# Transposing the ds tiles of an attention backward loop by three DMAs a block instead of two

## The chip, the cores and the metric

One core of a Trainium2 chip. The metric is the device time of one execution in microseconds (us). The engines: TensorE (PE in the profile, PEld its weight loads), VectorE (DVE), ScalarE (ACT), GpSimd (POOL), SyncE (SP). SyncE computes nothing here; it issues nearly all DMAs, one after the other, in program order.

## The reference, cut to what matters

A parallel block, attention plus a gated feed-forward, run forward and then differentiated:

```python
def _fwd_reference(A_x, ...):
    xn = _layernorm(A_x)
    return A_x + attention(xn, A_wqkv, A_wo) + swiglu(xn, B_w_gate, B_w_up, B_w_down)
# S = 2048 tokens, D = 448, H = 16 heads of 28, F = 1792
# result: the output, and the gradients of x and of five weights
```

The attention backward needs, for each head and each pair of a query tile and a key chunk, `ds` (the gradient of the scores) twice: as it is, for dk, and transposed, for dq.

## The kernel before: the parts concerned

The backward loop runs 512 steps. A step is one query tile of 128 rows against a key chunk of 512 columns for two heads; four steps (qi = 0 to 3) are a block. `row` makes the score and dP matmuls. `ew` makes exp on ScalarE and `ds` on VectorE, into buffers that hold two tiles each:

```python
def dst_dma(b, ds, qi):
    if qi == 2:
        SP.dma_start_transpose(out=dsT[b][:, 2]..., in_=ds[:, 0]...)        # one tile, L826
        return
    dsT[b] = bk.tile([P, 4, 2, 4, P], BF16, name="dsT", bufs=3)
    SP.dma_start_transpose(out=dsT[b][:, 0:2]..., in_=ds[:]...)             # two tiles, L830

def ew(k):
    ...                                                                     # exp
    if qi % 2 == 0:
        dss[k - 1] = dss[k] = kq.tile([P, 2, 2, 512], BF16, name="ds_sb", bufs=5)
    ds = dss[k - 1]
    for j in range(2):
        DVE.tensor_tensor(out=ds[:, qi % 2, j], in0=dps..., in1=est..., op=ALU.mult)   # L845
    if qi == 1 or qi == 2 and b < NB // 4 - 1:
        dst_dma(b, ds, qi)
```

Tile 3 of a block is transposed on TensorE instead (`tr_unit`, L900). `dq_unit(b)` uses all four transposed tiles ten steps after tile 2 was written. With five buffers, a ds buffer is written again when the fifth newer pair of tiles comes, and that write must wait until the DMA has read the old tiles.

The same SyncE queue carries the loop's other traffic: prefetch loads "dripped" in at some 100 KB a step (L767) and stores of results (L800).

```python
def drop():                       # once a step
    ...
    while slow and credit > 0:
        _, _, o, i = slow.pop(0)
        SP.dma_start(out=o, in_=i)
        credit -= size(o)
```

One ds tile is 128 x 1024 bf16, 256 KB; a typical load piece is 256 KB too.

The softmax here doesn't subtract the row's maximum and nothing guards it: scores larger than these inputs give would overflow.

## Time and profile before

| | before |
|---|---|
| median of 3 runs | 1472.74 us (1466.82 to 1473.25) |
| PE, ACT, DVE busy | 91%, 86%, 79% of the span |
| backward loop, block 0 to 126 | 789.8 us, 6.27 us a block |
| two-tile issue / one-tile issue on SyncE, median | 3.04 / 1.25 us |

A "block" is timed in the trace from the end of one block's fourth ds multiply (of eight, two a tile; the fourth completes tile 1) to the next block's. An issue's duration is how long SyncE is held by it, not how long the data move: in the queue kernel of experiment 1 the two-tile issue at 29.03 us held SyncE for 1.84 us, and its last packet started 3.76 us after it. The lines themselves are in the prediction below.

### The profile page before, as it was taken

The numbers are of one execution on the slowest core, as the hardware profiler recorded it, in microseconds if no ns is written. First come the engines' busy times: TensorE is split into PE (matmuls) and PEld (weight loads), VectorE is DVE, ScalarE is ACT, GpSimd is POOL, SyncE is SP. The second block draws the span as 40 slices with busy tenths as digits, with TensorE's granted clock in tenths as the row PEclk, the third lists the DMA queues.
The fourth block names the chain that finished last, engine by engine and source line by source line (L and its number), as shares of the span: only waits on it lengthen the run. The fifth ranks groups of instructions, "written<-read, shape, count | busy, mean of one in ns | idle before, by whom it ended". The sixth has DMA issues, their size and how long they took to land. (4 is left out here: it accounts for less than half of the span.)

```text
span 1468.9 us, 34341 instructions
## 1 busy us (share of the span) xinstructions
PE 1338.7 (91%) x12647; PEld 544.8 (37%) x12708; DVE 1153.9 (79%) x1997; ACT 1262.4 (86%) x2193; POOL 361.8 (25%) x486
## 2 busy tenths in 40 slices
PE   5889999989999999888899989999999999999996
PEld 2333333333333333333333433433343444344343
DVE  6667756656667767497888878888889999899988
ACT  5789988988989998687888879899989999888974
POOL 6464514553344444010001101101001011010005
PEclk9999999999999999998999999999999999999998
DMA  5797957696778685699999999999999999999961
GB/s 151 147 210 179 223 118 179 165 197 155 167 160 190 145 184 125 206 198 199 214 204 196 214 204 189 210 203 216 212 195 194 206 217 217 199 194 206 193 140 59
DMA packets 697664, 271.14 MB, mean 185 GB/s; under 512 B 616128, under 2 KB 672152, under 8 KB 697496
## 3 DMA queue, kind: packets, MB, share of 16 engines
q1 hardware_dynamic: 692520, 262.82, 86.7%
q0 software_dynamic: 3568, 5.83, 1.8%
q8 instruction: 100, 1.64, 0.5%
q14 instruction: 68, 0.56, 0.1%
q10 hardware_dynamic: 1408, 0.30, 0.1%
HBM read 65.04 MB, written 59.90 MB: 85 GB/s over the span
## 5 line engine op out<-in xcount | busy, mean ns | idle before, releaser
L845 DVE TENSOR_TENSOR ds_sb<-db,e_sb 128x512 bf16<-128x512 f32 x1024 | 648.4, 685 | 68.6 <-PE db L818 22.6
L837 ACT ACTIVATE e_sb<-sb 128x512 bf16<-128x512 f32 x1024 | 554.1, 609 | 60.3 <-PE db L818 43.8
L611 ACT ACTIVATE eT<-s_w 128x1024 bf16<-128x1024 f32 x256 | 263.7, 1030 | 48.6 <-PE s_ps L608 45.8
L613 ACT ACTIVATE eT<-s_ps 128x512 bf16<-128x512 f32 x512 | 280.2, 611 | 0.0
L818 PE MATMUL db<-kd,qd 32*128 32x512 bf16 x1024 | 239.9, 385 | 19.5 <-DVE ds_sb L845 18.7
L810 PE MATMUL sb<-kd,qd 32*128 32x512 bf16 x1024 | 210.9, 389 | 7.5 <-DMA qd<-QD_d 3.7
L964 POOL TENSOR_TENSOR dq_acc<-dq_acc,dq_st 128x256 f32<-128x256 f32 x64 | 46.4, 724 | 588.6 <-ACT dq_st L962 588.6
L905 ACT COPY dsT<-db 128x1024 bf16<-128x1024 bf16 x128 | 130.0, 1016 | 37.1 <-PE db L900 36.5
L922 PE MATMUL acc<-ds_sb,qd 128*32 128x512 bf16 x1024 | 161.4, 392 | 0.0
L918 PE MATMUL acc<-e_sb,qd 128*32 128x512 bf16 x1024 | 159.4, 392 | 1.3 <-DVE dw_o L527 1.3
L379 POOL TENSOR_TENSOR nn<-nn,ag 128x512 f32<-128x512 f32 x56 | 71.2, 1272 | 253.9 <-DVE ag L377 245.4
L608 PE MATMUL s_ps<-QQ,KK 32*128 32x512 bf16 x512 | 125.5, 385 | 3.9
L1132 PE MATMUL genb<-wguT,dau_c 128*128 128x448 bf16 x448 | 117.5, 355 | 6.3 <-ACT dq_st L962 3.8
L608 PE MATMUL s_w<-QQ,KK 32*128 32x512 bf16 x512 | 100.3, 387 | 13.2 <-ACT eT L611 10.2
L810 PEld LDWEIGHTS <-qd 32*128 32x128 bf16 x1024 | 48.3, 91 | 152.6 <-issue 140.6
L420 PE MATMUL gen<-xn_t,f_sp 128*128 128x448 bf16 x416 | 91.8, 354 | 2.6 <-DVE nn L394 1.7
L949 PE MATMUL genb<-dsT,kd 128*32 128x256 bf16 x2048 | 80.9, 279 | 3.5 <-DVE y L1084 1.8
L420 PEld LDWEIGHTS <-f_sp 128*128 128x128 bf16 x640 | 55.7, 98 | 76.4 <-issue 31.7
L900 PE MATMUL db<-ident_bf,ds_sb 128*128 128x128 bf16 x1032 | 82.1, 225 | 0.9 <-DVE ds_sb L845 0.9
L900 PEld LDWEIGHTS <-ds_sb 128*128 128x128 bf16 x1032 | 70.6, 101 | 28.6 <-issue 10.3
L450 PE MATMUL gen<-eT,VS 128*32 128x512 bf16 x1024 | 68.0, 382 | 6.0 <-DVE nn L394 3.8
L380 POOL TENSOR_TENSOR nn<-nn,tt 128x512 f32<-128x512 f32 x56 | 72.0, 1286 | 4.4
(163 smaller groups left out, 1872.0 us busy)
## 6 DMA issues: line engine op xcount, KB each, us to landing
F_d<-hda SPq DMA_DIRECT2D x56, 384.0 KB
dau_c<-F_d SPq DMA_DIRECT2D x56, 256.0 KB
h_c<-F_d SPq DMA_DIRECT2D x24, 256.0 KB
qd<-QD_d SPq DMA_DIRECT2D x24, 256.0 KB
dc<-dqkvT_d SPq DMA_DIRECT2D x12, 384.0 KB
dsT<-ds_sb SPq DMA_TRANSPOSE x255
wT_d<-wT_f SPq DMA_DIRECT2D x14, 256.0 KB
KD_d<-qk_sp SPq DMA_DIRECT2D x7, 512.0 KB
```

The source lines that it names most:

```text
L420: PE.matmul(ps[:, :D], lhsT=fsp[fc][:, t // 4, w, t % 4, :], rhs=rhs[:, t, :], start=(t == 0), stop=(t == NT - 1))
L608: PE.matmul(sp4[hh], lhsT=KK[g][r:r + HP, kt * P:(kt + 1) * P], rhs=QQ[g][r:r + HP, qsl], start=True, stop=True, tile_position=(r, 0))
L611: ACTE.activation(out=e2[0][:], in_=wide[:], func=ACT.Exp, scale=SCALE)
L613: ACTE.activation(out=e2[1][:, j], in_=sp4[2 + j], func=ACT.Exp, scale=SCALE)
L810: PE.matmul(s_ps[:], lhsT=qside[g, qc][r:r + HP, 0, qi * P:(qi + 1) * P], rhs=kside[g, kc][r:r + HP, 0, :], start=True, stop=True, tile_po ...
L818: PE.matmul(d_ps[:], lhsT=qside[g, qc][r:r + HP, 1, qi * P:(qi + 1) * P], rhs=kside[g, kc][r:r + HP, 1, :], start=True, stop=True, tile_po ...
L837: ACTE.activation(out=est[k][:, j], in_=sps.pop((k, j))[:], func=ACT.Exp, scale=SCALE)
L845: DVE.tensor_tensor(out=ds[:, qi % 2, j], in0=dps.pop((k - 1, j))[:], in1=est[k - 1][:, j], op=ALU.mult)
L900: PE.transpose(ps[:, c, :], ds[:, qi % 2, c // 4, (c % 4) * P:(c % 4 + 1) * P], ident_bf[:])
L905: ACTE.copy(out=o, in_=ps[:])
L918: PE.matmul(a[r:r + HP, :], lhsT=sp4[:, 1, r:r + HP], rhs=e[:, j, :], start=first, stop=last, tile_position=(0, r), skip_group_check=True)
L922: PE.matmul(a[r:r + HP, :], lhsT=sp4[:, 0, r:r + HP], rhs=ds[:, qi % 2, j, :], start=first, stop=last, tile_position=(0, r), skip_group_ch ...
```

## The change

Its intent: each of the three tiles goes out as soon as it is written, so its transpose starts earlier and its buffer is free earlier. It costs one more DMA a block. The bytes, the matmuls and the transposes on TensorE stay the same.

```diff
     def dst_dma(b, ds, qi):
-        if qi == 2:
-            SP.dma_start_transpose(out=dsT[b][:, 2]..., in_=ds[:, 0]...)
-            return
-        dsT[b] = bk.tile([P, 4, 2, 4, P], BF16, name="dsT", bufs=3)
-        SP.dma_start_transpose(out=dsT[b][:, 0:2]..., in_=ds[:]...)
+        if qi == 0:
+            dsT[b] = bk.tile([P, 4, 2, 4, P], BF16, name="dsT", bufs=3)
+        SP.dma_start_transpose(out=dsT[b][:, qi]..., in_=ds[:, qi % 2]...)
 ...
-            if qi == 1 or qi == 2 and b < NB // 4 - 1:
+            if qi < 2 or qi == 2 and b < NB // 4 - 1:
```

More of the change, by code (lines that the diff above doesn't have):

```diff
@@ L824, in dst_dma @@
     def dst_dma(b, ds, qi):
-        if qi == 2:
-            SP.dma_start_transpose(out=dsT[b][:, 2].rearrange("p j kt s -> p (j kt) s"),
-                                   in_=ds[:, 0].rearrange("p j k -> p (j k)"))
-            return
-        dsT[b] = bk.tile([P, 4, 2, 4, P], BF16, name="dsT", bufs=3)
-        SP.dma_start_transpose(out=dsT[b][:, 0:2].rearrange("p q j kt s -> p (q j kt) s"),
-                               in_=ds[:].rearrange("p q j k -> p (q j k)"))
+        if qi == 0:
+            dsT[b] = bk.tile([P, 4, 2, 4, P], BF16, name="dsT", bufs=3)
+        SP.dma_start_transpose(out=dsT[b][:, qi].rearrange("p j kt s -> p (j kt) s"),
+                               in_=ds[:, qi % 2].rearrange("p j k -> p (j k)"))
     def ew(k):
```

## The prediction

> **What bounds the kernel now.** I read four views in this order: the page's slices, the waits of VectorE, windows around the longest of those waits, and the timeline of SyncE's DMA issues.
>
> The change touches only the backward attention loop, which runs from about 620 to 1430 us: 128 blocks of four query tiles, some 6.27 us a block ((1414.0 - 624.2) us between the same multiply of block 0 and block 126, over 126). The slices say that TensorE, ScalarE and the DMA engines are all nearly full there.
>
> ```profile
> PE   5889999989999999888899989999999999999996
> DVE  6667756656667767497888878888889999899988
> ACT  5789988988989998687888879899989999888974
> PEclk9999999999999999998999999999999999999998
> DMA  5797957696778685699999999999999999999961
> ```
>
> A tuned loop like this is not set by one engine. What the change can win is what TensorE loses to DMA, so I ask who waits for the transposes. Of VectorE's waits from 620 to 1430 us (total us, times, longest us):
>
> ```profile
> DVE ds_sb L845 <- PE db L818: 22.6, 57, 1.7
> DVE ds_sb L845 <- DMA dsT<-ds_sb: 15.9, 11, 2.5
> ```
>
> The second line is the one: the multiply that writes a ds tile stood still 11 times because the transposing DMA had not yet read what lay in that buffer before. The longest eight of these waits lie at 668, 680, 690, 711, 768, 854, 888 and 1262 us: mostly the first third of the loop. The worst one, first TensorE's timeline, then windows around it (busy us of each engine, granted clock, DMA share, GB/s):
>
> ```profile
> 665.51 0.39 PE L818 MATMUL db<-kd,qd 32*128 32x512 bf16 x1
> 668.56 0.58 PE L818 MATMUL db<-kd,qd 32*128 32x512 bf16 x1 [2.66 <-DVE ds_sb L845]
> ```
>
> ```profile
> 640.00:667.00 27.00, 24.52 (x295) 11.50 (x292) 22.96 (x38) 25.37 (x49) 0.72 (x1) 1.00 0.99 201
> 667.00:674.00 7.00, 5.40 (x46) 2.02 (x46) 3.87 (x7) 3.31 (x6) 0.23 (x1) 0.52 0.91 185
> 674.00:740.00 66.00, 58.41 (x623) 23.52 (x623) 54.49 (x89) 54.24 (x100) 7.01 (x10) 0.95 1.06 206
> ```
>
> VectorE's wait becomes 2.66 us of TensorE idle, and then the granted clock falls from 1.00 to 0.52 for 7 us. Windows over 711 to 715, 769 to 773, 854 to 858 and 1264 to 1268 us each show 0.57, right behind the waits at 711, 768, 854 and 1262. So a wait for a transpose is paid about twice.
>
> Why are the transposes late? SyncE issues them; L830 is two tiles in one DMA, L826 one tile:
>
> ```profile
> 652.81 0.57 SPq L767 DMA_DIRECT2D wd_sb<-in_B_w_down_dram  x1
> 653.43 0.48 SPq L767 DMA_DIRECT2D h_c<-F_d  x1
> 654.01 3.21 SPq L830 DMA_TRANSPOSE dsT<-ds_sb  x1
> 657.27 1.43 SPq L800 DMA_DIRECT2D out_dram<-dqT  x2
> 658.80 2.03 SPq L826 DMA_TRANSPOSE dsT<-ds_sb  x1
> 660.92 0.52 SPq L800 DMA_DIRECT2D dqkvT_d<-dkv  x1
> 661.50 0.97 SPq L767 DMA_DIRECT2D h_c<-F_d  x2
> 662.57 3.27 SPq L830 DMA_TRANSPOSE dsT<-ds_sb  x1
> ```
>
> There is no hole between these lines: SyncE's queue is full. The two tiles that go out at 662.57 us were ready at 653.85 us (end of block 5's fourth multiply), so the queue is 8.7 us behind its data. Followed in the timeline from block to block, this lag grows from 2.6 us (block 0) to 13.0 us (block 7), is cut by VectorE's waits, stands at 5 to 11 us up to 880 us, rises again near 1060 and 1255 us, and is 0.03 us from 1350 us on. The rows of the two lines give min/median/max in ns:
>
> ```profile
> L830 SPq DMA_TRANSPOSE dsT<-ds_sb x128: 1746/3044/4773, 626.8 to 1419.8; - x128
> L826 SPq DMA_TRANSPOSE dsT<-ds_sb x127: 1232/1252/2486, 629.8 to 1415.9; - x127
> ```
>
> One tile costs 1.25 us nearly always; two together cost not 2.5 but 3.04.
>
> **What the Trainium skill says.** "Perfetto Trace Analysis", section "DMA Instruction — HWDGE (DVE, Sync)": the profiled window runs from satisfied semaphores to a free sequencer, so it is descriptor generation, not data movement, and the DMA engines start before it is over when more descriptors are made than the buffer holds. That fits: two tiles alone in a quiet queue take 1.75 us, behind copies in flight up to 4.77 us, as if the issue must wait until part of itself has drained, while one tile fits. The same page, "What 'DMA-bound' means": a sequencer track that is solid DMA slices is a bound of its own. The trace agrees from 640 to 720 us: issues fill 96% of SyncE's time. The same page, "DMA Optimizations", has it both ways: batch small transfers, yet splitting may let some start sooner if the DMA engines are generally idle. They are not idle here (slices of 9), which is the case against the change. "TensorE: Matmul & The Clock Gate", "What's actually happening": an idle window of about 3.4 us halves the clock. The trace agrees on the halving, though 2.66 us of idle was enough.
>
> **The change part by part.**
> 1. Removed: per block one two-tile issue. Added: two one-tile issues. The same bytes in the same 256-byte packets move. At the medians: 2 x 1.25 - 3.04 = -0.54 us of SyncE time a block. Per block from 640 to 720 us: before, 3.26 (mean of L830 there) + 1.34 (mean of L826) + 3.1 copies x 0.56 + 5 gaps of 0.05 = 6.6 us, against some 5.87 us that blocks 1 to 7 took before the waits began; so the lag must grow 0.7 us a block. After: 3 x 1.30 (mean of one-tile issues, my choice between 1.25 and 1.34) + 1.74 + 0.30 = 5.9 us: even with the block. From 720 to 900 us the same sum gives 3.12 + 1.48 + 1.45 + 0.25 = 6.3 before and about 5.7 after. The lag stops growing and mostly vanishes.
> 2. Moved: the first tile's transpose is asked for one step (about 1.4 us) earlier, and the second no longer ends with its partner. By the code, the buffer that held tiles 0 and 1 is written again nine steps later (about 13.2 us). Minus 3.3 us of issue and an assumed 2.2 us until landed, a lag of 7.7 us is tolerated now; with 1.25 us of issue, 9.8 us.
> 3. Added: the dsT tile is taken one step earlier, before the dq matmuls of three blocks back are issued in the same step, so SyncE may wait for those 16 matmuls (1.07 us in the timeline at 672 us), which run while VectorE still works on the ds tile. Off the path: SyncE then waits for VectorE in any case. Two more semaphore updates per block cost nothing on a computing engine.
>
> What the waits cost now, from the length of blocks (5.87 us where undisturbed): blocks 8 to 14 took 52.8 us instead of 41.1 (11.7 lost), block 23 lost 3.6, block 25 lost 2.0 (behind a late store of y), block 36 lost 3.3, block 102 lost 3.5. Sum 24 us, about the 15.9 us of waits plus half of the roughly 24 us of half clock, less overlap. I expect 60% back, since at 205 GB/s in a first third full of loads some of the delay is the DMA engines' own: 0.6 x 24 = 14.5 us. 1472.7 - 14.5 = 1458 us.
>
> **The rivals.**
> A. The issue is throttled by the DMA engines, not by the size of an instruction: then three issues share the same 4.6 us a block, 1.5 each, and the lag grows as before. For it: DMA share 0.99 to 1.16 in windows of the loop, and one-tile issues of 1.7 to 1.9 us directly behind a two-tile issue near 1396 us. Against: one-tile issues under full load stay at 1.25. Only the tolerance of part 2 is won: 3 to 6 us, 1467 to 1470 us.
> B. Everything comes back: no waits, no clock dips, and stores and loads that trail SyncE (a 2.2 us wait for kd at 854 us) are in time too: 24 to 28 us, 1445 to 1449 us. Against it: the heavy loads of the first blocks remain.
> C. A new wait: the earlier dsT claim, or more DMAs in flight behind SyncE's recycled semaphores (every issue waits on its own), holds the queue and the loads behind it. Where SyncE has no lag, this could cost up to 0.1 us a block, 1475 to 1485 us. Against: from 1350 us on SyncE has idle time, and ahead of that its lag hides it.
>
> **How range and chances follow.** Centre 1458 from the sum; A and B set 1445 and 1472 as the ends of the range. Over 2% faster means under 1443.3 us, more than all that I can find lost: chance 0.07. Over 2% slower would need C in every block: 0.03. Within 2%: 0.90.
>
> **What would show it.** If right: the wait "DVE ds_sb <- DMA dsT" falls from 15.9 us to under 6; one-tile issues (382 of them on one line) have a median near 1.25 us; the lag of SyncE behind the multiply stays under 8 us before 900 us; the half-clock dips at 667, 677, 711, 769, 854 and 1264 us mostly go; the gain lies before 900 us, with under 4 us after 1060 us outside the stretch around 1262. Wrong if one-tile issues have a median over 1.5 us (A), or if SyncE shows holes while VectorE waits for transposes (C).

## The result, and the profile after

The changed kernel took 1454.14 us (median of 4 runs, 1449.54 to 1457.57), against 1469.78 us for the kernel before in its 4 runs. The ratio is 0.9891, with a 95% interval of 0.985 to 0.9932. It is the mean time of one kernel's fast runs over that of the other's of the same rounds, so it is not quite the ratio of the medians. 1458 was predicted, and "within 2%" is what came.

First the waits of VectorE from 620 to 1430 us in the changed kernel (total us, times, longest us):

```profile
DVE y L1081 <- DMA out_dram<-y: 4.7, 3, 2.3
...
DVE ds_sb L842 <- DMA dsT<-ds_sb: 3.1, 4, 1.4
```

The wait for a transpose fell from 15.9 to 3.1 us. The waits for the stores of y, 2.4 us in all before, are now VectorE's largest for a DMA. SyncE's queue in the loaded first third:

```profile
654.91 1.23 SPq L827 DMA_TRANSPOSE dsT<-ds_sb  x1
656.20 0.91 SPq L767 DMA_DIRECT2D h_c<-F_d  x1
657.20 1.23 SPq L827 DMA_TRANSPOSE dsT<-ds_sb  x1
658.48 1.05 SPq L800 DMA_DIRECT2D out_dram<-dqT  x2
659.63 1.23 SPq L827 DMA_TRANSPOSE dsT<-ds_sb  x1
660.91 0.58 SPq L767 DMA_DIRECT2D h_c<-F_d  x1
```

The queue is still solid, yet in this stretch the 3.2 us issues are gone, and loads and stores stand between the tiles. All the issues of the loop in one row (min/median/max ns); 37 of the 383 still took over 2 us:

```profile
L827 SPq DMA_TRANSPOSE dsT<-ds_sb x383: 1231/1265/3402, 621.9 to 1398.5; - x192
```

Where in the loop did the time come from? Windows over the same blocks, 0 to 14, 14 to 26 and 26 to 42, of the kernel before (start and end, length, busy us of PE, PEld, DVE, ACT and POOL, granted clock as a share of TensorE's full speed, DMA share, GB/s; the DMA share adds up the packets' times over 16 engines, so it can pass 1):

```profile
624.20:718.10 93.90, 80.56 (x857) 32.52 (x856) 75.04 (x123) 75.79 (x141) 9.50 (x13) 0.93 1.01 202
718.10:795.80 77.70, 71.10 (x795) 29.71 (x794) 67.45 (x111) 66.79 (x124) 5.80 (x8) 0.98 1.07 204
795.80:900.00 104.20, 94.16 (x1052) 39.16 (x1051) 90.14 (x148) 89.13 (x165) 8.70 (x12) 0.97 1.06 204
```

and of the changed kernel:

```profile
619.30:707.30 88.00, 80.40 (x857) 31.71 (x856) 74.96 (x124) 75.29 (x140) 9.51 (x13) 0.90 1.06 210
707.30:784.80 77.50, 70.55 (x795) 29.07 (x794) 67.36 (x110) 67.00 (x124) 5.81 (x8) 0.98 1.10 215
784.80:884.50 99.70, 92.00 (x1052) 38.72 (x1051) 89.98 (x148) 88.69 (x165) 8.70 (x12) 0.98 1.12 207
```

In the first and third stretch the engines do the same work in less time; the second, blocks 14 to 26, is hardly shorter (77.7 and 77.5 us; 76.0 in the second profile below), and why is not shown. The DMA engines move their bytes at a higher rate (202 to 210 GB/s, 204 to 215, 204 to 207). Blocks 0 to 42 took 275.8 us before and 265.2 after: 10.6 us. Blocks 92 to 104 gave 3.1, the rest 2.7, so the loop gave 789.8 - 773.4 = 16.4 us. The two profiled executions differ by 21.2 us (1468.9 to 1447.7); the other 4.9 lie ahead of block 0, in code that the change does not touch. That part is from run to run: a second profile of the changed kernel (the control of experiment 7) reached block 0 at 623.8 us instead of 619.3. Its loop took 777.7 us, a gain of 12.1 instead of 16.4, and 10.9 of them before block 42. So a difference of a few us between two single profiles is noise, and the first third is where both show the gain.

### The profile page after: what moved, and what is told of

Its sections match the earlier page's. It is cut to its first block, busy times and chain, and to the rows that moved or that the text cites. A ratio compares the mean times of both kernels' runs of the same rounds, so it can differ in the third digit from the quotient of the medians.

```text
span 1447.7 us, 34917 instructions
## 1 busy us (share of the span) xinstructions
PE 1337.1 (92%) x12708; PEld 541.2 (37%) x12708; DVE 1153.0 (80%) x1997; ACT 1262.5 (87%) x2193; POOL 362.6 (25%) x486
## 5 line engine op out<-in xcount | busy, mean ns | idle before, releaser
L608 PEld LDWEIGHTS <-KK 32*128 32x128 bf16 x1024 | 28.8, 91 | 115.4 <-issue 112.0
```

The lines of the kernel that those rows point to most:

```text
L608: PE.matmul(sp4[hh], lhsT=KK[g][r:r + HP, kt * P:(kt + 1) * P], rhs=QQ[g][r:r + HP, qsl], start=True, stop=True, tile_position=(r, 0))
```

## The experiments

**1. The issues by themselves.** A kernel that computes nothing and only issues the loop's transposes and 256 KB loads, first one at a time, alone or after one or two loads, then in free-running streams of 16 blocks (the streams are shown). Its outputs are zeros.

```diff
+    for block in ((T2, LD, T1, LD, LD), (T1, LD, T1, LD, T1, LD), (T2, T1), (T1, T1, T1), (LD, LD, LD)):
+        for _ in range(16):
+            for f in block: f()       # T2, T1: transpose of two tiles, of one; LD: a load
```

> A kernel that computes nothing (its outputs are zeros on purpose): only the DMA issues of the loop, by themselves. Issue-size theory: on a quiet queue one tile costs about 1.24 us of SyncE and two tiles about 1.75; behind one or two 256 KB loads one tile stays near 1.25 while two tiles go to 3 us or more. In the free-running stream a block of two-tile, load, one-tile, load, load takes at least 0.3 us longer than a block of three one-tile issues and three loads. DMA-engine theory (rival A of the prediction): both streams take the same time a block within 0.1 us, since the same bytes move, and one-tile issues in the stream rise to 1.5 us or more.

The time of a block in each stream (first issue's start to last issue's end, over 16):

| stream | us a block | median issue of two tiles / one tile |
|---|---|---|
| two tiles, load, one tile, load, load | 6.41 | 3.32 / 1.23 |
| three times (one tile, load) | 5.79 | - / 1.23 |
| two tiles, one tile | 3.84 | 1.74 / 1.96 |
| three times one tile | 4.13 | - / 1.33 |
| three loads | 1.89 | |

The two mixed streams in the timeline of SyncE, first with two tiles together, then with single tiles:

```profile
240.13 3.67 SPq L136 DMA_TRANSPOSE dsT<-ds  x1
243.84 0.58 SPq L148 DMA_DIRECT2D ld<-in_A_wqkv_dram  x1
244.47 1.23 SPq L142 DMA_TRANSPOSE dsT<-ds  x1
245.74 1.06 SPq L148 DMA_DIRECT2D ld<-in_A_wqkv_dram  x2
```

```profile
303.00 1.23 SPq L142 DMA_TRANSPOSE dsT<-ds  x1
304.27 0.58 SPq L148 DMA_DIRECT2D ld<-in_A_wqkv_dram  x1
304.89 1.23 SPq L142 DMA_TRANSPOSE dsT<-ds  x1
306.17 0.61 SPq L148 DMA_DIRECT2D ld<-in_A_wqkv_dram  x1
```

With loads between, the single tiles are 0.63 us a block quicker, with no engine to compute and nothing that the issues wait for (some 0.05 us lie between them). The rival that only the bytes count is out. Without loads it is the other way round: together is 0.29 us quicker. So one DMA for two tiles is not slow in itself; it is slow behind loads. One part of the expectation was not tested. The two-tile issues that were to stand directly behind one or two loads took 1.87 and 1.84 us, not 3; but each of them first waited until its source tile had been written again, and by then the last load packet had ended 0.8 to 1.1 us earlier (one load), or between 0.5 us earlier and 0.1 us later (two loads). They were quiet queues once more. In the stream, the second two-tile issue already took 3.52 us.

The packet records fit the reading that such an issue is held until part of itself has drained. Of the issue at 285.4 us the first packet starts 2.0 us later, after load packets, and 791 of its 2048 packets have started when SyncE is free again; over the 15 held issues of that stream it is 560 to 1085. A single tile in the same stream set SyncE free before any of its 1024 packets had started. That is a reading, not a proof of where the limit sits.

**2. Two single tiles, but both late.** The second kernel cuts the two-tile DMA in two and leaves it where it was.

```diff
-        SP.dma_start_transpose(out=dsT[b][:, 0:2]..., in_=ds[:]...)
+        for q in range(2):
+            SP.dma_start_transpose(out=dsT[b][:, q]..., in_=ds[:, q]...)
```

> The two tiles go out as two DMAs but both only when the second is written, as before. Issue-size theory: most of the gain stays, ratio to before 0.988 to 0.993, VectorE waits for transposes 3 to 7 us. Early-start theory (the gain is that tile 0 is asked for a step earlier): ratio 0.997 to 1.003, waits as before, some 16 us.

1457.55 us against 1470.7; ratio 0.9913 (0.9887 to 0.9938). VectorE waited 9.2 us for transposes, more than the 3 to 7 expected. Most of the gain needs no earlier start. Whether the earlier start adds the last 0.2% cannot be told: the intervals overlap.

**3. One more buffer instead of the split.** If VectorE's wait for a ds buffer were the cost itself, a sixth buffer should be worth as much as the change.

```diff
-   dss[k - 1] = dss[k] = kq.tile([P, 2, 2, 512], BF16, name="ds_sb", bufs=5)
+   dss[k - 1] = dss[k] = kq.tile([P, 2, 2, 512], BF16, name="ds_sb", bufs=6)
# and, for room: gs, pr and dx of the last stage with 1, 1 and 2 buffers
```

> The kernel before with six ds buffers instead of five (and three small buffers of the last stage cut, to make room). If what the late transposes cost is only VectorE's wait for a ds buffer and the clock dips behind it: waits for transposes under 3 us, ratio 0.985 to 0.991, as good as the change, although the issues are still 3.0 and 1.25 us and the lag still grows past 9 us. If the lag costs by other ways too (late loads and stores, late dsT tiles for the dq matmuls): ratio 0.993 to 1.0.

1467.22 against 1470.7 us; ratio 0.9979 (0.9953 to 1.0005): no gain clear of the noise. The smaller buffers do not hide one: what follows block 126 took 55.4 us, 54.9 before. The waits of this kernel:

```profile
PE genb L949 <- DMA dsT<-ds_sb: 6.4, 6, 2.1
...
DVE y L1084 <- DMA out_dram<-y: 6.0, 2, 3.5
...
PE sb L810 <- DMA kd<-KD_d: 2.8, 1, 2.8
DVE dwq_o L1021 <- DMA out_dram<-dwq_o: 2.5, 1, 2.5
```

VectorE's wait for transposes is gone altogether, and most of the time is not. The lateness turns up elsewhere: the dq matmuls wait for transposed tiles (6.4 us, none before), VectorE for the store of y (6.0, was 2.4) and of dwq (2.5, was 0.8), TensorE for a key load (2.8, was 2.2). The wait that I had named as the cost looks like only the place where a full queue showed first.

**4. Halves.** Each tile cut again, six DMAs a block.

```diff
-        SP.dma_start_transpose(out=dsT[b][:, qi]..., in_=ds[:, qi % 2]...)
+        for j in range(2):
+            SP.dma_start_transpose(out=dsT[b][:, qi, j], in_=ds[:, qi % 2, j])
```

> Each tile's transpose is cut again, into two DMAs of half a tile: six issues a block. Issue-size theory: a fixed part near 0.7 us is paid six times (6 x 1.0 = 6 us and copies on top, against a block of 5.9 us), SyncE becomes the bound of the loop: lag over 9 us almost everywhere, VectorE waits 40 us or more, ratio 1.02 to 1.10. DMA-engine theory: issues only wait for the same bytes, so ratio 0.985 to 1.0, like the change.

1904.86 us, ratio 1.2953 (1.2907 to 1.2999): the direction of the issue-size theory, and far past its size, because half a tile costs SyncE as much as a whole one:

```profile
L828 SPq DMA_TRANSPOSE dsT<-ds_sb x766: 1188/1216/2733, 624.9 to 1856.5; - x192
```

The tile issues of a block (7.53 us) and its copies (1.34) fill 8.87 us of SyncE; a block took 9.61. VectorE waited 241 us for transposes over the whole loop, which here runs to 1857 us. So one tile a DMA is the best of the three cuts tried: half a tile pays the fixed cost twice, two tiles are held behind loads.

**5. More orders in the queue alone.**

```diff
+    for block in (..., (T1, T1, LD, T1, LD, LD), (LD, LD, LD, T2, T1), (LD, LD, LD, T1, T1, T1), ...):
```

> No arithmetic (outputs are zeros on purpose): more orders of the same three tiles and three 256 KB loads a block, free running. Known: two tiles, load, one tile, load, load took 6.41 us a block; three single tiles each followed by a load 5.79. If the size of the issue decides: one, one, load, one, load, load takes 5.7 to 5.9, and three loads followed by two tiles and one tile take 6.3 or more. If it is the alternation of loads and tiles that helps: one, one, load, one, load, load takes 6.2 or more, and three loads followed by three single tiles too.

| order in a block | us a block |
|---|---|
| two tiles, load, one tile, load, load | 6.30 |
| one, one, load, one, load, load | 6.11 |
| three loads, two tiles, one tile | 6.64 |
| three loads, one, one, one | 6.41 |
| two tiles, load, load, one tile, load | 6.31 |
| one, load, one, load, one, load | 5.80 |

Neither theory alone has it. The first order had taken 6.41 in experiment 1, so 0.1 us is what two runs differ by. Cutting the two tiles without moving a load is worth 0.2 us a block (6.30 to 6.11, 6.64 to 6.41); putting a load between all tiles is worth 0.3 more (6.11 to 5.80). The change does the first, and much of the second: its timeline above shows loads and stores between tiles.

**6. The same loads issued by GpSimd.** To take time off SyncE without touching the tiles:

```diff
-            SP.dma_start(out=o, in_=i)          # in drop()
+            POOL.dma_start(out=o, in_=i)
```

> The kernel before, with the prefetch loads that are dripped into the loop issued by GpSimd instead of SyncE (two-tile issues kept). If SyncE's own time is what is short (6.6 us of issues a block against 5.9), taking some 1.5 us a block away from it ends the lag: waits for transposes under 4 us, ratio 0.982 to 0.993. If the two-tile issue is slow because loads stand before it in the DMA engines, whoever issued them, and that is what counts: issues stay near 3 us, ratio 0.995 to 1.005. GpSimd's own adds may be held up by its waits for buffers; then it can be over 1.005.

1514.48 us, ratio 1.0318 (1.0281 to 1.0355). SyncE had 11 copies to issue from 640 to 720 us instead of 39, and its two-tile issues still took 3.2 us in the median of the loop and up to 12.3. In those 80 us they took 4.26 on average instead of 3.26, and SyncE was 99% full. VectorE waited 38.6 us for transposes, where the theory of SyncE's time asked for under 4. That fits loads in the DMA engines, whoever issued them, as what holds such an issue. But GpSimd also stood waiting for free load buffers (36.6 us in one wait) with its own adds behind it, so the time of this run settles nothing between the theories.

**7. Fewer loads, with and without the split.** The loads of h for the second to fourth chunk are left out (the first output is wrong; the other six are right). They belong to the first half of the loop, but not to its first 14 blocks, whose loads stay.

```diff
+        if ch > 0:
+            h_c = ych[0, half]
+        else:
             h_c = yp.tile([P, NH, 512], BF16, name="h_c", bufs=3)
             drip(("y", ch, half), ...)
```

> The kernel before, but the loads of h for the second to fourth chunk are left out and the first chunk's are used again (the first output is wrong on purpose): 5.5 MB of loads less in the first half of the loop, everything else the same. If the first third of the loop runs at the pace of the DMA queue: VectorE waits for transposes under 5 us, blocks 0 to 42 fall from 6.57 to about 6.1 us a block, ratio 0.984 to 0.991 without any split. If the two-tile issue is itself too slow, loads or not: ratio 0.996 to 1.0.

> The same loads left out of the changed kernel. If the split helps only where loads stand between the transposes (in the queue by itself three single tiles take 4.13 us without loads, two and one take 3.84): the split is worth much less here than with the loads, under 0.5 per cent between this and the light kernel before. If the split helps in every surrounding: another 1.0 to 1.3 per cent below the light kernel before.

> The change itself, as a control on the same chip as the next two. Ratio to before 0.987 to 0.992 under every theory.

All three ran on one chip beside the kernel before (1470.29 us). The change again: 1455.98 us, ratio 0.9894 (0.986 to 0.9928). Light before: 1458.63 us, 0.9919 (0.9896 to 0.9943). Light with the split: 1447.8 us, 0.9845 (0.9821 to 0.987). Blocks 0 to 14, 14 to 26 and 26 to 42 of the light kernel before, as in the windows above:

```profile
621.30:715.80 94.50, 83.74 (x857) 32.54 (x856) 75.24 (x123) 75.52 (x140) 9.53 (x13) 0.87 1.01 200
715.80:789.40 73.60, 70.06 (x795) 29.56 (x794) 67.34 (x110) 66.81 (x124) 5.81 (x8) 0.98 1.04 195
789.40:885.10 95.70, 90.24 (x1052) 38.23 (x1051) 90.02 (x148) 88.41 (x165) 8.72 (x12) 1.00 1.05 185
```

and of the light kernel with the split:

```profile
622.80:712.20 89.40, 80.72 (x857) 31.90 (x856) 75.12 (x124) 74.88 (x140) 9.53 (x13) 0.90 1.06 208
712.20:787.30 75.10, 70.80 (x795) 29.79 (x794) 67.50 (x110) 67.21 (x124) 5.81 (x8) 0.95 1.08 198
787.30:882.60 95.30, 89.87 (x1052) 38.16 (x1051) 89.93 (x147) 88.36 (x165) 8.71 (x12) 1.00 1.06 185
```

This is the clearest pair, though of one profile each. Where the loads were cut, the split is worth nothing: 73.6 and 75.1 us in blocks 14 to 26, 95.7 and 95.3 in blocks 26 to 42. With all loads it was 77.7 and 77.5 there (no gain either), and 104.2 and 99.7. Where the loads stayed (blocks 0 to 14) the split is worth 5.1 us here as it was worth 5.9 with all loads. The expectations for the light kernel before were missed: VectorE still waited 10.6 us for transposes (not under 5), blocks 0 to 42 took 6.28 us each (not 6.1), and the ratio lies just above its range. The split was worth 0.9845 / 0.9919 = 0.7%, not under 0.5, where each ratio is known to about 0.25%. In these profiles the rest lies in stretches that kept their loads, blocks 0 to 14 and 92 to 104 (4.1 us, of which 2.4 because this light kernel was slower there than the full one).

**8. Looking for more.** Four y buffers on top of the change, against its longest remaining wait; then six ds buffers as well.

```diff
-            y = yp.tile([P, D], BF16, name="y")
+            y = yp.tile([P, D], BF16, name="y", bufs=4)
```

> The change plus four buffers for the output tile y instead of two. In the changed kernel VectorE's longest remaining waits for a DMA are for the store of y (4.7 us in 3 waits, clock dips behind two of them). If these cost as the ds waits did: that wait goes to zero and the ratio to before falls by 0.2 to 0.5 per cent against the change's 0.989, to 0.984 to 0.987. If they only hide another wait: 0.988 to 0.991.

> The change plus six ds buffers plus four y buffers (three small buffers of the last stage cut, to make room). No VectorE wait for a DMA over 1 us should be left in the loop; ratio 0.980 to 0.986, the best of all. If the lag just moves to the next taker (dsT for the dq matmuls, kd), as it did with six ds buffers without the change: 0.986 to 0.990.

1451.76 us, ratio 0.9884 (0.9868 to 0.99), and 1453.79 us, ratio 0.9903 (0.9889 to 0.9916), where the change has 0.9891 and 0.9894 in other rounds. The named waits did go to zero (y; y and ds), the time did not follow: with both, the dq matmuls wait 3.1 us for transposes and TensorE 2.5 us for a key load. Neither is shown to beat the change.

## Why the prediction was right, and where it was not

**The time and its place: right.** 14.5 us were promised and the medians show 15.6. That the size fits is in part luck: the 60% was a guess, applied to a sum that does not hold (below). Of the 16.4 us in the profiled loop 10.6 came before block 42 (885 to 900 us) and 3.1 in the stretch around the 1262 us wait; outside that stretch the last part, from block 72 on, gave 1.4 us.

**Part 1, SyncE's time: right.** "3 x 1.30" a block from 640 to 720 us measured 3 x 1.33. The saving there is 4.60 - 3.98 = 0.62 us a block, and the queue by itself shows the same 0.63. It shrinks where fewer issues are held: 4.58 to 4.32 us from 900 to 1060 us, nothing from 1060 to 1300. Rival A asked for a median over 1.5 us and got 1.265.

**"The lag stops growing and mostly vanishes": wrong.** In blocks 8 to 15 SyncE's issues started behind the end of their tile's multiply (the lag) by 8.0 to 8.7 us on average after the change, against 7.4 (the pair) and 9.3 (the single tile) before, and the worst lag after was 12.1 us, where I had asked for under 8. I had held the block at 5.9 us and let the queue catch up. What fits the traces is that the loop speeds up until the queue is behind again: where the queue sets the pace, its gain appears as shorter blocks (6.71 to 6.28 us in blocks 0 to 14), not as a shorter lag. It does not set the pace in every loaded stretch: in blocks 14 to 26 the transposes took some 5 us less of SyncE's time and the blocks were hardly shorter.

**Part 2, the tolerance: right as far as it goes.** Lags of 8 to 12 us now cost 3.1 us of waiting, where such lags had cost 15.9. But the sixth buffer shows that tolerance without a faster queue is worth little: 3.1 us, where the interval runs from a gain of 7 us to a loss of 1. Rival A's "3 to 6 us" for it is neither confirmed nor excluded by that.

**Part 3, the earlier dsT claim: right.** In the 15 blocks in which SyncE was idle when tile 0 was written, the dq matmuls it might have waited for had ended 0.1 to 0.5 us earlier each time.

**"A wait for a transpose is paid about twice": not borne out.** Between 640 us and the last stage the clock was at half for 30.7 us before and 13.7 us in the first profile of the changed kernel, which looks like the mechanism; but the second profile of the same changed kernel has 30.7 us again, and its loop is still 12.1 us shorter than before. So fewer dips are not what most of the gain is. They may cost something (the profile with 17 us more of half clock has the loop longer by 4.3 us), but that is one pair of profiles. The dips vary from run to run; the 24 us that I counted as lost, dips included, had the right size for another reason, a slower queue.

**What stays open:** whether the earlier start of tile 0 is worth 0.2% by itself, why blocks 14 to 26 gained next to nothing (0.2 and 1.7 us in the two profiles), and what exactly inside the DMA path holds a two-tile issue.

## What to carry to other kernels

When one queue carries both transposes and loads and is full, ask how long each instruction holds the queue in its real surroundings, not alone: here the larger DMA was the quicker one by itself and the slower one behind loads. Cut to the size whose issue is not held, not below the fixed cost of one, and let the kinds alternate. A wait for a buffer behind such a queue can be a symptom: here a further buffer moved it to the next taker.

## What the Trainium skill lacked or had wrong

- "DMA: Bandwidth & Descriptors", section "Rules for kernel authors", advises to coalesce many small transfers into one large one and speaks of sizes under 64 KB. At 256 and 512 KB, above that size, it still holds for transposes alone (3.84 us a block together, 4.13 apart); with loads between it turns round (6.41 together, 5.79 apart), which the page does not say.
- No page gives what a DMA transpose from SBUF to SBUF costs the issuing sequencer on this chip by its size and by what stands before it in the queue; "DMA: Bandwidth & Descriptors" has a single cycle count, for one large transfer on "previous generations". Here: 1.22 us for half a tile (128 KB, in the loop), 1.23 for one (256 KB), 1.3 to 2.0 for two on a quiet queue, 3.3 in a full stream with loads.
- "Perfetto Trace Analysis", section "DMA Optimizations", ties splitting to DMA engines that are generally idle. Here their share was 1.0 or more in the loaded stretches and splitting still gave 1.1%, by a faster queue.
- "TensorE: Matmul & The Clock Gate", section "What's actually happening", speaks of an idle window of about 3.4 us. Here no gap in TensorE's timeline was that long in the loop, and half clock still came: behind single gaps of 1.4 to 2.7 us, but also at 659.6 us of the changed kernel, where the 7 us before show two gaps of 0.23 us, while a gap of 1.47 us at 785.6 us before the change brought none. Two profiles of one kernel had 13.7 and 30.7 us of half clock in the same stretch.
